# Top-32 attention with an MLP behind it: eight candidates of the smaller halves instead of sixteen, a second computation behind a branch, and 16 more units turned by VectorE

## The chip, the cores and the metric

The kernel runs on one core of a Trainium2 chip. A core has five instruction streams that matter here. TensorE (PE in the profile, with its weight loads as PEld) multiplies matrices. VectorE (DVE) does element-wise work, transposes of 32x32 blocks, and two special instructions for a top-k search: MAX8 gives the eight largest values of each row, and MATCH_REPLACE8 overwrites those eight in place. ScalarE (ACT) applies functions and copies out of PSUM. GpSimd (POOL) does element-wise work in SBUF. SyncE (SP) issues most DMAs. Each engine runs its own instructions in the order of the program, and semaphores hold an instruction until the others have produced what it reads. The metric is the device time of one execution in microseconds (us), as the median of several runs.

## What is computed

Eight batches, eight heads, 576 positions, head size 64, all in float32. For each row of the scores the 32nd largest is found, everything below it is masked, and the rest goes through a softmax and is multiplied with the values. The heads are then laid side by side and pass through a layer norm and an MLP with a hidden width of 2048 and a residual.

```python
scores = scale * np.matmul(q, k.transpose(0, 1, 3, 2))
kth = np.partition(scores, -top_k, axis=-1)[..., -top_k:-top_k + 1]     # top_k = 32
scores = np.where(scores >= kth, scores, -1000000000.0)
attn = np.exp(scores - np.max(scores, axis=-1, keepdims=True))
attn = attn / (np.sum(attn, axis=-1, keepdims=True) + 1e-09)
x = heads_side_by_side(np.matmul(attn, v))
xn = (x - mu) / np.sqrt(var + 1e-06) * g_ln
out = x + np.maximum(xn @ w_ch1, 0.0) @ w_ch2
```

## The kernel before

**Units.** The attention is cut into 160 units. A unit is a pair of heads of one batch with 128 query rows (a whole unit, two tiles of 128 rows by 576 keys, one for each head), or the last 64 rows of both heads in one tile (a rest unit). There are 128 whole units and 32 rest units, 288 tiles in all. Units are collected in groups of two or three that share their transposed weights `pt` and are multiplied with the values together.

**Top 32 of a row.** A row of 576 scores is folded: `halve` (L421) takes the larger of columns i and i+288 into `hi` (L433, on VectorE) and the smaller into `lo`. The smaller is made on GpSimd by two integer operations on the bits: a minus the larger, plus b (L438 and L441); only unit 0 uses a plain minimum on VectorE (L436). `select` (L443) then searches in four parts. Part 0 takes the sixteen largest of `lo` (MAX8 L453, MATCH_REPLACE8 L448, MAX8 L453) and puts them behind `hi`, which so gets 304 columns. Parts 1 to 3 run four rounds of MAX8 (L462) over the 304 columns with three rounds of MATCH_REPLACE8 (L448) between them. The last value of the fourth round is the 32nd largest of the row.

**Mask and softmax weights.** `mask` (L486) is one ScalarE instruction with the function Prelu and a slope of 2^-90 on the side of the values that are kept, so that kept and dropped values differ by a factor of 2^90. `weigh` (L493) is the exponential, with a scale that undoes the slope and a bias from `prepare` (L470: on VectorE for the first units, on GpSimd by two tiny operations, L483 and L484, from unit `CONVERTING` on); it sums the row as it goes.

**Turning the weights.** The weights have to be transposed for the product with the values. For most units TensorE does it with transposing matmuls (L553, L582), and ScalarE copies the result out of PSUM (L565, L583). For 72 units, those of batches 2 to 7 that are not a rest unit and not the last of their group, VectorE does it (`move`, L525: two STREAM_TRANSPOSE at L531 that write over the scores tile `sc`), and SP sends the blocks to HBM by one DMA (`turned`) and back into `pt` by four.

**Order.** The order is written out by hand. The program is a loop over steps; in step n each engine gets, in this order, the exponential of the first tile of unit n-2, the scores of unit n+2 (the products L412 on TensorE, four copies L393 to `sc` on ScalarE), the product of an older group with the values (L607, L614), the four parts of `select` for unit n, `halve` of unit n+1 between parts 1 and 2, and the two masks of unit n-1. During the first 8 units (`EARLY`) mask and exponential of a unit both stand in the same step, mask, exponential, mask, exponential. Matmuls of the MLP (L752, L909) are the filler: a list `todo` is spread over eight slots of a step. Up to `CONVERTING` a slot's share is the planner's VectorE cost of the step (`DVE_UNIT` 8.6 for a whole unit) less its TensorE cost; later it is what is left, spread evenly over the steps. In the first 17 or so steps the weights of the MLP are also converted, two pieces in a step: three or four ScalarE operations, a clamp on GpSimd (L197), a shift on VectorE (L200), and an addition and a product on GpSimd (L206, L208).

**Buffers.** Scores tiles `sc` have five buffers, `hi` two, `lo` one, the weights `e` two, `pt` one. The queues of the engines hold: on GpSimd the preparation of unit n-1, the halves of unit n+1, the sums of the MLP's blocks (L839 to L845, L889, L893, L723).

## Time and profile before

| what | us |
|---|---|
| time, median of 3 runs | 1653.51 (1651.67 to 1654.98) |
| time of the profiled execution | 1652.03 |
| span of the profiled execution | 1650.0 |
| TensorE busy | 1504.6 (91% of the span) |
| VectorE busy | 1458.2 (88%) |
| ScalarE busy | 1064.0 (64%) |
| GpSimd busy | 958.4 (58%) |
| mean granted TensorE clock | 0.959 of full speed |

A reader should look at three stages and not at the shares of the whole. Up to about 200 us the weights are converted and TensorE has little to do. From there to about 1490 us the 160 units run, with the MLP's matmuls as filler. After that VectorE is done with its units, and TensorE works off the last blocks of the MLP almost without a pause. In the lists below a row gives the source line, the engine, the operation, what it writes and reads, how often it ran, then busy time, mean duration of one, and the idle time before it with what ended it.

### The profile page before, as it was taken

The page shows a single profiled execution, that of the slowest core. Times are in us where ns is not written, and L with a number is a line of the kernel's source. Part 1 is how long each engine was busy: PE and PEld are TensorE (multiplying, and loading weights), DVE is VectorE, ACT ScalarE, POOL GpSimd, SP SyncE. Part 2 cuts the span into 40 slices and gives each one's busy share as a digit, 9 for nine tenths or more (in the row PEclk, how much of TensorE's full clock was granted, in tenths as well). Part 3 has the DMA queues.
Part 4 walks back from the last instruction along what each step waited for, and adds up shares of the span by engine and source line. Part 5 has one row for each costly group of instructions (what it writes and reads, how often), then busy time and mean ns, then how long its engine had stood idle before and what let it go on. Part 6 is the DMA issues. An engine that isn't in the chain of part 4 may idle for free.

```text
span 1650.0 us, 27871 instructions
## 1 busy us (share of the span) xinstructions
PE 1504.6 (91%) x7897; PEld 1134.6 (69%) x7897; DVE 1458.2 (88%) x4652; ACT 1064.0 (64%) x2712; POOL 958.4 (58%) x1492
## 2 busy tenths in 40 slices
PE   3569998999888988999999998999989999999998
PEld 1336566767655766777677776777767777778887
DVE  5999898999999999999999999999999999994000
ACT  6987876767655756667566665676657766654411
POOL 4778759555555564656564656474646564655243
PEclk6679999999999999999999999999999999999999
DMA  7533355113454455535555456535564455532211
GB/s 200 131 128 114 100 119 143 55 58 90 124 156 136 124 144 160 159 94 139 171 165 162 114 128 177 168 105 135 153 184 134 130 131 169 154 114 83 73 51 51
DMA packets 358945, 211.46 MB, mean 128 GB/s; under 512 B 250756, under 2 KB 331144, under 8 KB 358792
## 3 DMA queue, kind: packets, MB, share of 16 engines
q1 hardware_dynamic: 354056, 209.10, 44.9%
q10 hardware_dynamic: 4736, 0.59, 0.3%
q8 instruction: 63, 1.03, 0.3%
q14 instruction: 90, 0.74, 0.2%
HBM read 145.62 MB, written 63.96 MB: 127 GB/s over the span
## 4 chain that ended last, share of the span: by engine, by line
DVE 65%; PE 19%; POOL 7%; ACT 3%; DMA 2%; issue 2%; SPq 1%; DVEq 0%; POOLq 0%; ACTq 0%
DVE m L462 19%; DVE hi L448 17%; DVE hi L453 10%; PE hps L752 8%; PE ops L909 6%; DVE lo L448 6%; DVE hi L433 5%; DVE sc L531 4%; PE av L607 2%; PE scps L412 1%; POOL lo L441 1%; POOL lo L438 1%; DVE st L677 1%; DVE kT L342 1%; POOL w L208 1%
## 5 line engine op out<-in xcount | busy, mean ns | idle before, releaser
L752 PE MATMUL hps<-xT,w 128*128 128x256 f32 x2304 | 547.5, 383 | 1.9 <-ACT xT L714 1.9
L462 DVE MAX8 m<-hi 128x8 f32<-128x304 f32 x1152 | 489.5, 462 | 3.3
L752 PEld LDWEIGHTS hps<-xT,w 128*128 128x128 f32 x2304 | 422.0, 191 | 71.6 <-issue 15.4
L438 POOL TENSOR_TENSOR lo<-sc,hi 128x576 int32<-128x576 int32 (+1 forms) x159 | 204.5, 1286 | 451.3 <-DVE hi L433 224.3
L448 DVE MATCH_REPLACE8 hi<-m,hi 128x304 f32<-128x304 f32 x864 | 391.1, 460 | 0.0
L909 PE MATMUL ops<-w,h 128*128 128x256 f32 x1360 | 325.6, 383 | 1.7 <-POOL h L845 1.7
L909 PEld LDWEIGHTS ops<-w,h 128*128 128x128 f32 x1360 | 248.6, 191 | 42.9 <-issue 6.9
L453 DVE MAX8 hi<-lo 128x8 f32<-128x288 f32 x576 | 234.2, 443 | 7.5 <-POOL lo L441 6.4
L393 ACT COPY sc<-scps 128x288 f32<-128x288 f32 x576 | 195.8, 409 | 58.2 <-PE scps L412 21.0
L499 ACT ACTIVATE e<-e,bias 128x576 f32<-128x576 f32 x288 | 225.5, 783 | 9.6 <-POOL bias L484 9.0
L489 ACT ACTIVATE e<-sc,m 128x576 f32<-128x576 f32 x288 | 225.0, 782 | 5.8 <-DVE m L462 3.2
L441 POOL TENSOR_TENSOR lo<-lo,sc 128x576 int32<-128x576 int32 (+1 forms) x159 | 204.3, 1285 | 12.5
L607 PE MATMUL av<-pt,vb 128*64 128x256 f32 (+2 forms) x1088 | 158.1, 435 | 47.2 <-DMA pt<-turned 24.5
L607 PEld LDWEIGHTS av<-pt,vb 128*64 128x64 f32 x1088 | 81.6, 149 | 115.4 <-issue 42.2
L775 ACT ACTIVATE h<-hps 128x512 f32<-128x512 f32 x144 | 86.1, 598 | 115.8 <-PE hps L752 115.3
L412 PE MATMUL scps<-kT,late_qT 64*128 64x288 f32 (+3 forms) x832 | 128.7, 411 | 7.9 <-ACT pt L565 5.3
L909 PE MATMUL ops<-wt,s 128*128 128x256 f32 x544 | 129.2, 381 | 0.0
L448 DVE MATCH_REPLACE8 lo<-hi,lo 128x288 f32<-128x288 f32 x288 | 125.6, 443 | 0.0
L531 DVE STREAM_TRANSPOSE sc<-e 128x512 f32<-128x512 f32 x144 | 93.8, 685 | 35.0 <-ACT e L499 34.9
L433 DVE TENSOR_TENSOR hi<-sc 128x576 f32<-128x576 f32 (+1 forms) x160 | 110.8, 692 | 10.0 <-ACT sc L393 10.0
L553 PE MATMUL tp<-ident,e 128*128 128x128 f32 x576 | 91.7, 284 | 29.9 <-ACT e L499 28.3
L412 PE MATMUL scps<-kT,qT 64*128 64x288 f32 x512 | 92.3, 461 | 27.9 <-DVE qT L342 26.1
(96 smaller groups left out, 1843.9 us busy)
## 6 DMA issues: line engine op xcount, KB each, us to landing
turned<-sc SPq DMA_DIRECT2D x72, 512.0 KB, 2.6
pt<-turned SPq DMA_DIRECT2D x288, 128.0 KB, 2.9
w<-forms SPq DMA_DIRECT2D x136, 256.0 KB, 3.8
vb<-in_v_dram SPq DMA_DIRECT2D x136, 128.0 KB, 3.2
raw<-in_moe_w_ch_dram SPq DMA_DIRECT2D x32, 512.0 KB, 4.2
kT<-kept SPq DMA_DIRECT2D x36, 288.0 KB, 3.3
kin<-in_k_dram SPq DMA_DIRECT2D x128, 72.0 KB, 2.5
kept<-kT SPq DMA_DIRECT2D x32, 288.0 KB, 3.1
```

Source lines behind the costliest of these rows:

```text
L393: nc.scalar.copy(u.sc[:, t, s * HALF : (s + 1) * HALF], made[s][t][:, 0:HALF])
L412: nc.tensor.matmul(ps[i * R : i * R + ql, o : o + width], qT[r, q0 : q0 + ql], kT[r, k0 : k0 + width], start=True, stop=True,)
L438: nc.gpsimd.tensor_tensor(lo.bitcast(I32), a.bitcast(I32), hi.bitcast(I32), ALU.subtract)
L441: nc.gpsimd.tensor_tensor(lo.bitcast(I32), lo.bitcast(I32), b.bitcast(I32), ALU.add)
L448: nc.vector.match_replace(x[:, t], m[:, t, :], x[:, t], LOWEST)
L453: nc.vector.max(u.hi[:, t, o : o + 8], u.lo[:, t])
L462: nc.vector.max(m[:, t, :], u.hi[:, t])
L489: nc.scalar.activation(u.e[:, t], u.sc[:, t], AF.Prelu, bias=u.thr[:, t, 7:8], scale=-1.0, alpha=SLOPE)
L499: nc.scalar.activation(u.e[:, t], u.e[:, t], AF.Exp, bias=u.bias[:, t : t + 1], scale=-scale / SLOPE, accum_out=g.den[:, col : col + 1],)
L607: nc.tensor.matmul(av[h * D : (h + 1) * D, 0 : g.nq], vb[:, h * J + c, :], g.blocks[:, h, 0 : g.nq // 32, c, :], start=(c == 0), stop=False,)
L752: nc.tensor.matmul(ps[0][:, side * N : (side + 1) * N], w1[:, c, f * P : (f + 1) * P], self.xT[:, c, 0:N], start=(c == 0), stop=(c == NC - 1),
L909: nc.tensor.matmul(bank[name][:, 0:Q], a(j), rhs, start=first and j == 0, stop=(j == G - 1), skip_group_check=not first,)
```

## The change

The top-level function becomes `compute`, with two new arguments: `low_rounds`, the number of rounds over `lo`, and `doubt`, a one-element tile or nothing. The new top-level function calls it with one round, loads `doubt` into a register on every engine, and calls it again, with two rounds and no doubt, inside a branch that is taken only where `doubt` is 1. So the program holds two whole computations, one after the other.

- The search takes eight candidates of `lo` instead of sixteen: one MAX8 and no MATCH_REPLACE8 on `lo`. The first two rounds over `hi` now run on 288 columns, the last two on 296 (all four had 304).
- `halve` makes the smaller halves with a plain minimum on VectorE for every unit; GpSimd's two integer operations are gone.
- `mask` becomes a ScalarE Relu with a slope of 2^90 followed by a subtraction of the scores on GpSimd over the whole tile; the exponential reads the result. In the first 8 units the two masks now stand ahead of the two exponentials.
- `watch` notes for each unit, with one tiny operation, whether the eighth candidate reaches the row's 32nd value; every 16 units two short reductions on VectorE collect it (`settle_watch`), and at step N `tell` brings it to one number, with one transpose on TensorE.
- Bias and threshold of the mask are written into unused columns of the last round's tile, by two tiny operations as before.
- VectorE turns all units from `EARLY` on that are not a rest unit and not the last of their group: 88, of which 16 are new (4 of batch 0, 12 of batch 1).
- `DVE_UNIT` in the planner becomes 7.65 and the rest unit's cost 0.58 of that. Two small tiles change pools.

```diff
     nt = len(u.tiles)
     u.lo = lopool.tile([P, 2, HALF], FP32, tag="lo", name="lo")
-    u.hi = hipool.tile([P, 2, HALF + TOP_K // 2], FP32, tag="hi", name="hi")
+    u.hi = hipool.tile([P, 2, HALF + 8 * low_rounds], FP32, tag="hi", name="hi")
     nc.vector.tensor_tensor(hi, a, b, ALU.max)
-    if u.i == 0:
-        nc.vector.tensor_tensor(lo, a, b, ALU.min)
-        return
-    nc.gpsimd.tensor_tensor(lo.bitcast(I32), a.bitcast(I32), hi.bitcast(I32), ALU.subtract)
-    nc.gpsimd.tensor_tensor(lo.bitcast(I32), lo.bitcast(I32), b.bitcast(I32), ALU.add)
+    nc.vector.tensor_tensor(lo, a, b, ALU.min)
...
 def select(u, i):
-    if i == 0:
-        for o in range(HALF, HALF + TOP_K // 2, 8):
-            for t in nt:
-                nc.vector.max(u.hi[:, t, o : o + 8], u.lo[:, t])
-            if o == HALF:
-                for t in nt:
-                    replace(u.hi[:, :, o : o + 8], t, u.lo)
-        return
-    for r in ((0,), (1,), (2, 3))[i - 1]:
-        ...
+    if i == 1:
+        for r in range(low_rounds):
+            o = HALF + 8 * r
+            for t in nt:
+                nc.vector.max(u.hi[:, t, o : o + 8], u.lo[:, t])
+            ...
+    width = HALF + 8 * low_rounds if i > 1 else HALF
+    for t in nt:
+        nc.vector.max(m[:, t, :], u.hi[:, t, 0:width])
+    if i < TOP_K // 8 - 1:
+        for t in nt:
+            replace(m, t, u.hi[:, t, 0:width])
...
 def prepare(u):
+    u.bias, u.edge = u.thr[:, 0:nt, 5], u.thr[:, 0:nt, 6]
+    if doubt is not None:
+        watch(u)
+    eng = nc.vector if u.i < CONVERTING else nc.gpsimd
+    eng.tensor_scalar(u.edge, u.thr[:, 0:nt, 7], STEEP, 0.0, ALU.mult, ALU.add)
+    eng.tensor_scalar(u.bias, u.top[:, 0:nt, 0], -scale, 0.0, ALU.mult, ALU.add)
...
+def watch(u):
+    c = 1 + 2 * (u.i % 16)
+    eng = nc.vector if u.i < CONVERTING else nc.gpsimd
+    eng.tensor_tensor(watched[:, c : c + nt], u.hi[:, 0:nt, HALF + 7], u.thr[:, 0:nt, 7], ALU.subtract)
...
 def mask(u, t):
     nc.scalar.activation(
-        u.e[:, t], u.sc[:, t], AF.Prelu, bias=u.thr[:, t, 7:8], scale=-1.0, alpha=SLOPE
+        u.e[:, t], u.sc[:, t], AF.Relu, bias=u.edge[:, t : t + 1], scale=-STEEP
     )
+    nc.gpsimd.tensor_tensor(u.e[:, t], u.e[:, t], u.sc[:, t], ALU.subtract)
...
-for u in units[jobs[5 * NHP].first :]:
+for u in units[EARLY:]:
     u.moved = not u.rest and u is not u.group.units[-1]
...
-DVE_UNIT, DVE_REST, DVE_MOVE, DVE_TURN = 8.6, 5.0, 1.4, 1.45
+DVE_UNIT = 6.0 + 1.65 * low_rounds
+DVE_REST, DVE_MOVE, DVE_TURN = 0.58 * DVE_UNIT, 1.4, 1.45
...
     if early:
         for t in range(2):
             mask(ex, t)
+        for t in range(2):
             weigh(ex, t)
...
+    if doubt is not None and at(n - 1) and at(n - 1).ends_watch:
+        settle_watch()
+        if n == N:
+            tell()
...
+    doubt = ctx.enter_context(tc.tile_pool(name="doubt", bufs=1)).tile([1, 1], I32, tag="doubt", name="doubt")
+    compute(tc, *operands, low_rounds=1, doubt=doubt[:])
+    again = nc.values_load(doubt[:], min_val=0, max_val=1, ...)
+    with tc.If(again > 0):
+        compute(tc, *operands, low_rounds=2, doubt=None)
```

More of the change, by code (lines that the diff above doesn't have):

```diff
@@ L19 @@
 DEN_EPS = 1.0e-9
-SLOPE = 2.0**-90
+STEEP = 2.0**90
 LN_EPS = 1.0e-6
@@ L29, with compute @@
 @with_exitstack
-def kernel(
+def compute(
     ctx: ExitStack,
@@ L39 @@
     out: bass.AP,
+    low_rounds: int,
+    doubt: bass.AP | None,
 ):
@@ L136 @@
         nc.gpsimd.memset(t[:], 0.0)
+    if doubt is not None:
+        watched = const([P, 34], "watched")
+        nc.gpsimd.memset(watched[:], -1.0)
     ident = const([P, P], "ident")
@@ L372, in __init__ @@
             self.tiles = [(0, 1)] if self.rest else [(0,), (1,)]
-            self.moved = False
+            self.moved = self.ends_watch = False
             self.e = None
@@ L433, in halve @@
         nc.vector.tensor_tensor(hi, a, b, ALU.max)
-        if u.i == 0:
-            nc.vector.tensor_tensor(lo, a, b, ALU.min)
-            return
-        nc.gpsimd.tensor_tensor(
-            lo.bitcast(I32), a.bitcast(I32), hi.bitcast(I32), ALU.subtract
-        )
-        nc.gpsimd.tensor_tensor(lo.bitcast(I32), lo.bitcast(I32), b.bitcast(I32), ALU.add)
+        nc.vector.tensor_tensor(lo, a, b, ALU.min)
     def select(u, i):
@@ L447, in replace @@
         def replace(m, t, x):
-            nc.vector.match_replace(x[:, t], m[:, t, :], x[:, t], LOWEST)
-        if i == 0:
-            for o in range(HALF, HALF + TOP_K // 2, 8):
+            nc.vector.match_replace(x, m[:, t, :], x, LOWEST)
+        if i == 1:
+            for r in range(low_rounds):
+                o = HALF + 8 * r
                 for t in nt:
                     nc.vector.max(u.hi[:, t, o : o + 8], u.lo[:, t])
-                if o == HALF:
+                if r < low_rounds - 1:
@@ L455, in select @@
                     for t in nt:
-                        replace(u.hi[:, :, o : o + 8], t, u.lo)
-            return
-        for r in ((0,), (1,), (2, 3))[i - 1]:
-            pl = brief_small if r in (1, 2) else small
-            m = pl.tile([P, 2, 8], FP32, tag=f"m{r}", name=f"m{r}")
-            for t in nt:
-                nc.vector.max(m[:, t, :], u.hi[:, t])
-            if r < TOP_K // 8 - 1:
-                for t in nt:
-                    replace(m, t, u.hi)
-            if r == 0:
-                u.top = m
-            u.thr = m
+                        replace(u.hi[:, :, o : o + 8], t, u.lo[:, t])
@@ L470, in prepare @@
+        width = HALF + 8 * low_rounds if i > 1 else HALF
+        pl = brief_small if i in (1, 2) else small
+        m = pl.tile([P, 2, 8], FP32, tag=f"m{i}", name=f"m{i}")
+        for t in nt:
+            nc.vector.max(m[:, t, :], u.hi[:, t, 0:width])
+        if i < TOP_K // 8 - 1:
+            for t in nt:
+                replace(m, t, u.hi[:, t, 0:width])
+        if i == 0:
+            u.top = m
+        u.thr = m
     def prepare(u):
         nt = len(u.tiles)
-        u.bias = small.tile([P, 2], FP32, tag="bias", name="bias")
@@ L474, in prepare @@
-        b = u.bias[:, 0:nt]
-        if u.i < CONVERTING:
-            for t in range(nt):
-                nc.vector.tensor_scalar(
-                    b[:, t : t + 1], u.thr[:, t, 7:8], u.top[:, t, 0:1], scale,
-                    ALU.subtract, ALU.mult,
-                )
-            return
-        nc.gpsimd.tensor_tensor(b, u.thr[:, 0:nt, 7], u.top[:, 0:nt, 0], ALU.subtract)
-        nc.gpsimd.tensor_scalar(b, b, scale, 0.0, ALU.mult, ALU.add)
+        u.bias, u.edge = u.thr[:, 0:nt, 5], u.thr[:, 0:nt, 6]
@@ new lines, in prepare @@
+        if doubt is not None:
+            watch(u)
[3 more added lines that the diff above has]
+    def watch(u):
+        nt = len(u.tiles)
+        c = 1 + 2 * (u.i % 16)
+        eng = nc.vector if u.i < CONVERTING else nc.gpsimd
+        eng.tensor_tensor(
+            watched[:, c : c + nt], u.hi[:, 0:nt, HALF + 7], u.thr[:, 0:nt, 7], ALU.subtract
+        )
+        if u.i % 16 == 15 or u.i == N - 1:
+            u.ends_watch = True
@@ new lines, in settle_watch, with tell @@
+    def settle_watch():
+        for out, first, op in ((0, 0, ALU.max), (33, 1, ALU.min)):
+            nc.vector.tensor_reduce(
+                watched[:, out : out + 1], watched[:, first : first + 33],
+                mybir.AxisListType.X, op,
+            )
+    def tell():
+        w = hpool.tile([P, J * P], FP32, tag="h", name="tell")
+        nc.gpsimd.memset(w[:], 0.0)
+        nc.vector.tensor_scalar(w[:, 1:2], watched[:, 33:34], -1.0e38, None, ALU.is_le)
+        nc.vector.tensor_scalar(w[:, 0:1], watched[:, 0:1], 0.0, None, ALU.is_ge)
+        nc.vector.tensor_tensor(w[:, 0:1], w[:, 0:1], w[:, 1:2], ALU.max)
+        ps = brief("tell")
+        nc.tensor.transpose(ps[:, 0:P], w[:, 0:P], ident[:])
+        nc.vector.tensor_reduce(w[0:1, P : P + 1], ps[0:1, 0:P], mybir.AxisListType.X, ALU.max)
+        nc.vector.tensor_copy(doubt, w[0:1, P : P + 1])
@@ L499, in weigh @@
         nc.scalar.activation(
-            u.e[:, t], u.e[:, t], AF.Exp, bias=u.bias[:, t : t + 1], scale=-scale / SLOPE,
+            u.e[:, t], u.e[:, t], AF.Exp, bias=u.bias[:, t : t + 1], scale=-scale,
             accum_out=g.den[:, col : col + 1],
@@ L675, in stats @@
                 self.rstd = small.tile([P, J], FP32, tag="rstd", name="rstd")
-            st = small.tile([P, 6], FP32, tag="st", name="st")
+            st = brief_small.tile([P, 6], FP32, tag="st", name="st")
             nc.vector.bn_stats(out=st[:], in_=x)
@@ L681, in stats @@
             else:
-                less = small.tile([P, 1], FP32, tag="less", name="less")
+                less = brief_small.tile([P, 1], FP32, tag="less", name="less")
                 nc.gpsimd.tensor_scalar(
@@ L1317, with kernel @@
             pop()
+@with_exitstack
+def kernel(
+    ctx: ExitStack,
+    tc: tile.TileContext,
+    *operands: bass.AP,
+):
+    nc = tc.nc
+    doubt = ctx.enter_context(tc.tile_pool(name="doubt", bufs=1)).tile(
+        [1, 1], I32, tag="doubt", name="doubt"
+    )
+    compute(tc, *operands, low_rounds=1, doubt=doubt[:])
+    again = nc.values_load(
+        doubt[:], min_val=0, max_val=1,
+        skip_runtime_bounds_check_because="a comparison's result",
+    )
+    with tc.If(again > 0):
+        compute(tc, *operands, low_rounds=2, doubt=None)
 _INS = ['q', 'k', 'v', 'moe_g_ln', 'moe_w_ch1', 'moe_w_ch2']
```

## The prediction

> **What bounds the kernel now.** I read the busy times first, then the stages, then the waits of the bound engine, then single rows.

> The page's busy line, then three stretches of the span: their length, the busy time of each engine in the order PE, PEld, DVE, ACT, POOL, the granted clock, DMA share and GB/s.

> ```profile
> PE 1504.6 (91%) x7897; PEld 1134.6 (69%) x7897; DVE 1458.2 (88%) x4652; ACT 1064.0 (64%) x2712; POOL 958.4 (58%) x1492
> ```

> ```profile
> 0.00:200.00 200.00, 132.82 (x582) 84.02 (x583) 172.44 (x566) 163.53 (x364) 143.90 (x136) 0.80 0.49 139
> 200.00:1490.00 1290.00, 1218.68 (x6564) 918.81 (x6563) 1267.83 (x4033) 851.58 (x2240) 750.40 (x1232) 0.98 0.48 135
> 1490.00:1650.00 160.00, 153.10 (x753) 131.79 (x753) 17.97 (x55) 48.88 (x110) 64.08 (x126) 0.99 0.21 63
> ```

> From 200 to 1490 us VectorE is busy 98.3% of the time (1267.8 of 1290) and TensorE 94.5% (1218.7). VectorE is the bound, but TensorE follows 49 us behind: whatever VectorE is spared beyond that is worth nothing in this stretch. Before 200 us TensorE idles for 67 us, and VectorE, ScalarE and GpSimd share the bound. After 1490 us TensorE alone works.

> What TensorE waits for between 500 and 1450 us, and what GpSimd waits for over the span (total, times, longest):

> ```profile
> PE av L607 <- DMA pt<-turned: 17.7, 10, 4.7
> PE av L607 <- ACT sc L393: 5.9, 2, 5.0
> PE av L607 <- DMA kept<-late_qT: 5.2, 1, 5.2
> ```

> ```profile
> POOL lo L438 <- DVE hi L433: 224.3, 64, 5.4
> POOL lo L438 <- DVE den L1238: 139.7, 54, 4.1
> ```

> TensorE's waits are mostly for data that VectorE delivered late, and should shrink with its load. The last two rows matter more than they seem: GpSimd waits for VectorE, behind its maximum, in most units, so it is idle while that maximum runs. The change removes this order.

> What it may cost shows in one place, around 254 us (the timeline: start, duration, engine):

> ```profile
> 253.83 1.28 POOL L962 TENSOR_TENSOR wt<-w 128x512 f32<-128x512 f32 x1
> ...
> 254.57 1.17 DVE L433 TENSOR_TENSOR hi<-sc 128x576 f32<-128x576 f32 x1
> 255.20 1.67 POOL L963 TENSOR_TENSOR wt<-w,wt 128x512 f32<-128x512 f32 x1
> ```

> Nearly every other maximum on 576 columns takes 0.74 to 0.76 us. This one starts while GpSimd runs an operation of the same kind, takes 1.17 us and ends 0.63 us after that operation, so that most of its own 0.75 lies behind it; GpSimd's next one takes 1.67 us where its like take 1.28. Two-input operations of the two engines seem to run one after the other.

> **The change, part by part.** Durations are from the groups of instructions, which follow.

> ```profile
> L462 DVE MAX8 m<-hi 128x8 f32<-128x304 f32 x1152 | 489.5, 462 | 3.3
> L448 DVE MATCH_REPLACE8 hi<-m,hi 128x304 f32<-128x304 f32 x864 | 391.1, 460 | 0.0
> L453 DVE MAX8 hi<-lo 128x8 f32<-128x288 f32 x576 | 234.2, 443 | 7.5 <-POOL lo L441 6.4
> L448 DVE MATCH_REPLACE8 lo<-hi,lo 128x288 f32<-128x288 f32 x288 | 125.6, 443 | 0.0
> L448 DVE MATCH_VALUE_LOAD lo<-hi,lo 128x8 f32 x288 | 22.8, 79 | 1.1
> L433 DVE TENSOR_TENSOR hi<-sc 128x576 f32<-128x576 f32 (+1 forms) x160 | 110.8, 692 | 10.0 <-ACT sc L393 10.0
> L531 DVE STREAM_TRANSPOSE sc<-e 128x512 f32<-128x512 f32 x144 | 93.8, 685 | 35.0 <-ACT e L499 34.9
> L553 PE MATMUL tp<-ident,e 128*128 128x128 f32 x576 | 91.7, 284 | 29.9 <-ACT e L499 28.3
> ```

> *Search.* One of two MAX8 over `lo` goes: 234.2/2 = 117.1 us. MATCH_REPLACE8 over `lo` goes with its loads: 125.6 + 22.8 = 148.4. Sixteen columns are worth 19 ns in a MAX8 (462 less 443) and 17 in a replacement, so the narrower `hi` saves 288 x (2x19 + 2x9.5 + 2x17 + 8.5) ns = 28.6. Sum 294.1 us of VectorE.

> *Minimum on VectorE.* As many and as large as the maximum: +110.8 us. Net of both, 183.3 us less over 160 units; 143 units are prepared by GpSimd after 200 us (its row at L483 counts 143), so 183.3 x 143/160 = 163.8 fall in the long stretch.

> *Sixteen more units turned.* VectorE +2 x 0.651 us each (93.8/144), 12 of them after 200 us: +15.6. TensorE loses eight transposes a unit, 91.7/576 = 0.159 each: 12 x 8 x 0.159 = 15.3 us. ScalarE loses 32 copies of 0.58, hidden before and after. SP gets five DMAs a unit, 80 of some 0.45 us; they land in 2.6 and 2.9 us, and the conversion's fetches queue behind them. A fetch is issued a step (10 us) ahead and lands in 4.2, so this costs nothing unless the step's end slips by 5 us.

> *Watch.* Every 16 units two reductions of some 0.2 us, +4 us on VectorE. One more 0.2 us operation a unit on GpSimd, +29. VectorE's maximum of unit n+1 now waits until GpSimd has watched unit n-1 (`hi` has two buffers). Behind it queue the whole next unit; GpSimd reaches the watch early in its step, so I take 0, the other end being the 2.6 us that its bias waited at most.

> *Mask.* GpSimd loses L438 and L441 (204.5 + 204.3 = 408.8) and gains 288 subtractions. The nearest row is its 576-column integer operation at 1.41 us: 406. So GpSimd's load stays. But each exponential now waits for GpSimd. In the steady part the subtraction stands half a step (4 to 5 us) ahead of its exponential: 0, as long as GpSimd is not that late. In the first 8 units it stands directly ahead: mask 0.78, subtraction 1.41, exponential; ScalarE waits about 0.65 and then 0.45 us, 1.1 a unit. From 60 to 110 us ScalarE is busy 47.2 of 50, 9.6 of a 10.2 us step, so its step becomes 10.7: +4 us over 8 steps, against up to 0.5 a step that VectorE saves in the next nine. I take +2 for the first 200 us, ends -8 and +12.

> *Side by side.* This is the large unknown. VectorE now runs two two-input operations a unit with GpSimd free to run beside them, busy about 0.6 of the time. The row above paid 0.42 us. A first operation meets GpSimd in 0.6 of cases and waits about half of an operation (0.5, over 1.41, 1.27 and 0.46 us operations): 0.3. The second either follows at once (0) or GpSimd, held back meanwhile, goes first (0.6 x 0.85 = 0.5): 0.25. I take 0.55 us a unit, 79 us over 143 units. Ends: 0, as in most rows now, and 2 x 0.6 x 1.41 = 1.7 us, 243 in all.

> [...]

> *Branch.* Each engine loads a register and jumps over a second program. No row shows it; the nearest are DMA landings of 2.4 to 5.1 us. I take +4, ends 0 and 10. In these inputs no row has more than six of its top 32 among the smaller halves, so the second computation should not run. [...]

> *Planner and tail.* The smaller `DVE_UNIT` and the moved units change the filler of steps 9 to 17 in opposite directions; the order of TensorE's matmuls is nearly the same. `tell` puts one transpose behind VectorE near the end: +2.

> **Sum.** VectorE in the long stretch: 1267.8 - 163.8 + 15.6 + 4 + 79 = 1203 us. TensorE: 1218.7 - 15.3 = 1203, less some 10 if half of its waits go, since the product with the values takes up to 4.5 us behind such a wait and 1.9 otherwise: 1193. Two engines with the same load that wait for each other fill less than 98.3% and more than 94.5%; with 96.5%, 1203 becomes 1246. So -44, and +2 +2 +4: 1650.0 - 36 = 1614 us of span. The profiled run took 2.0 more than its span and lies 1.5 under the median; I say **1615 us**. Its own range, with 0.3 to 0.8 us a unit, is 1592 to 1640.

> **Rivals.** *TensorE alone is the bound*: the engines hardly meet. VectorE needs 1124 us, TensorE 1193; at 98.5% that is 1211, and 1650 - 79 + 8 + 2 = **1581**. For it: TensorE hardly idles in the last stretch, where VectorE is out of the way. Against it: GpSimd is no longer held back by the maximum.

> *Waiting side by side costs more than the search saves* (slower). Without any gain VectorE could do 1282 x 0.983 = 1260 us, 136 more than 1124: break-even at 0.95 us a unit. At 1.2 us, 1296/0.983 = 1318, or 1650 + 28 + 8 + 2 = **1688**. For it: GpSimd's new 1.41 us operations. Against it: the single row paid 0.42.

> *GpSimd holds ScalarE*: exponentials wait in the steady part too, the scores' copies queue behind them and TensorE idles as now; 0.3 us a step in 150 steps eats the 44 and leaves the other 8: 1650 + 1 + 8 + 2 = **1661**. For it: the exponential waited for GpSimd's bias three times, up to 4.7 us, and GpSimd is busy 19.3 of 20 us around 250. Against it: 58% on average.

> **How the numbers follow.** Forecast 0.50, TensorE bound 0.25, side by side 0.18, GpSimd 0.07. The forecast is faster but for 0.03 that ends within 0.2%, TensorE's case always; the two others are slower: 0.72, 0.03 and 0.25. 0.2% (3.3 us) is about what a measurement can tell. The range takes in the forecast's own, most of TensorE's case and half of the slow one: 1568 to 1690 leaves out about a third of the 0.25 below and half of the 0.18 above, 0.17.

> **What the profile after would show.** [...] The maximum's and minimum's mean: 0.69 if they never meet GpSimd, 0.95 by my value, above 1.15 if slower. TensorE above 96% from 200 us on. Exponentials waiting for the subtraction: some 9 us early and few later. I am wrong if the mean of the two operations is off, or if ScalarE's waits for GpSimd exceed 40 us.

## The result

The changed kernel takes 1666.5 us, the median of four runs (1662.9 to 1669.3), against 1652.9 us of the kernel before on the same chip: 1.0084 times as long, with an interval of 1.0071 to 1.0096. It is 0.8% slower. I had forecast 1615 us and faster. The time lies inside my range, but on the other side of the kernel before.

The profiled execution took 1662.9 us, with a span of 1661.1. First the page's busy line after the change, then the same three stretches as in the prediction (length, busy time of PE, PEld, DVE, ACT and POOL, granted clock, DMA share, GB/s).

```profile
PE 1499.4 (90%) x7770; PEld 1124.9 (68%) x7770; DVE 1357.2 (82%) x4022; ACT 1051.2 (63%) x2680; POOL 1078.2 (65%) x1607
```

```profile
0.00:200.00 200.00, 120.91 (x484) 75.93 (x485) 160.79 (x458) 147.48 (x324) 133.59 (x121) 0.82 0.48 137
200.00:1490.00 1290.00, 1217.10 (x6494) 910.55 (x6493) 1173.23 (x3491) 850.74 (x2239) 862.98 (x1341) 0.98 0.50 147
1490.00:1650.00 160.00, 160.00 (x790) 137.52 (x789) 23.16 (x74) 51.77 (x116) 77.89 (x143) 1.00 0.23 68
```

VectorE lost its load as planned: in the long stretch it is busy for 1173.2 us instead of 1267.8, 91% of the time. But TensorE does no more there than before (1217.1 against 1218.7 us), and it does 12 us less in the first 200. No engine is busy all the time now; the engines wait for each other. The page's groups show for whom (busy time, mean ns of one, then the idle time before it and what ended most of it):

```profile
L484 POOL TENSOR_TENSOR e<-e,sc 128x576 f32<-128x576 f32 x288 | 411.6, 1433 | 418.1 <-ACT e L481 407.5
...
L429 DVE MAX8 m<-hi 128x8 f32<-128x296 f32 (+1 forms) x1152 | 465.0, 443 | 1.1
L415 DVE MATCH_REPLACE8 hi<-m,hi 128x288 f32<-128x288 f32 (+1 forms) x864 | 378.4, 444 | 0.0
...
L492 ACT ACTIVATE e<-e,m 128x576 f32<-128x576 f32 x288 | 225.0, 781 | 69.6 <-POOL e L484 69.2
L407 DVE TENSOR_TENSOR hi<-sc 128x576 f32<-128x576 f32 (+1 forms) x160 | 123.3, 771 | 142.1 <-POOL watched L452 120.8
...
L408 DVE TENSOR_TENSOR lo<-sc 128x576 f32<-128x576 f32 (+1 forms) x160 | 122.1, 763 | 0.0
L524 DVE STREAM_TRANSPOSE sc<-e 128x512 f32<-128x512 f32 x176 | 113.9, 682 | 7.4 <-ACT e L492 7.4
...
L421 DVE MAX8 hi<-lo 128x8 f32<-128x288 f32 x288 | 118.0, 446 | 0.0
L546 PE MATMUL tp<-ident,e 128*128 128x128 f32 x448 | 75.2, 294 | 47.1 <-ACT e L492 46.9
```

Read the last column as a ring. GpSimd's subtraction waits for ScalarE's mask (407.5 us; before, GpSimd waited for VectorE's maximum). ScalarE's exponential waits for GpSimd's subtraction (69.2). TensorE's transposes wait for the exponential (46.9; before 28.3). And VectorE's maximum waits for GpSimd's watch (120.8 us; before, this wait did not exist).

**How the loss builds up.** I took the start of the maximum of each unit from VectorE's timeline and subtracted its start in the kernel before. The differences in us, worked out so for several kernels (units 0 to 7 are the early ones):

| kernel | unit 5 | 10 | 23 | 47 | 79 | 119 | 151 |
|---|---|---|---|---|---|---|---|
| after | +2.6 | +19.3 | +23.5 | +31.1 | +19.4 | +13.9 | +10.8 |
| no_subtract_early | -1.7 | -1.9 | +1.5 | +10.1 | +3.5 | -1.8 | -4.2 |
| no_watch | +2.4 | +19.8 | +18.2 | +19.9 | -2.6 | -13.4 | -18.2 |
| neither_wait | -3.7 | -2.4 | -4.1 | +1.4 | -14.4 | -25.2 | -29.8 |
| no_guard_prelu | -3.8 | -2.8 | -16.6 | -28.3 | -50.0 | -61.4 | -66.9 |

After the change the kernel is 19 us late by unit 10, at about 140 us. It loses 12 more until unit 47 and wins 20 back until unit 151, where a kernel without guard and subtraction wins 67. The first place of the loss is the part in which mask, subtraction and exponential of a unit stand in one step. One such step from the timeline (start, duration, engine; in brackets the idle time before and what ended it):

```profile
96.37 1.46 ACT L481 ACTIVATE e<-sc,m 128x576 f32<-128x576 f32 x2
96.53 0.76 DVE L407 TENSOR_TENSOR hi<-sc 128x576 f32<-128x576 f32 x1 [3.05 <-ACT sc L367]
97.20 0.75 DVE L408 TENSOR_TENSOR lo<-sc 128x576 f32<-128x576 f32 x1
97.24 3.33 POOL L484 TENSOR_TENSOR e<-e,sc 128x576 f32<-128x576 f32 x2 [1.30 <-ACT e L481]
...
99.24 0.78 ACT L492 ACTIVATE e<-e,m 128x576 f32<-128x576 f32 x1 [1.42 <-POOL e L484]
...
100.17 1.11 PE L546 MATMUL tp<-ident,e 128*128 128x128 f32 x4 [4.70 <-ACT e L492]
...
100.61 0.78 ACT L492 ACTIVATE e<-e,m 128x576 f32<-128x576 f32 x1 [0.50 <-POOL e L484]
```

The scores' copies release ScalarE's masks and VectorE's two halves within 0.2 us of each other, so in this step, and in the last five of the eight early ones, GpSimd's subtractions begin while VectorE is at the minimum. The two take 3.33 us together, where twice the usual 1.41 would be 2.8. The first exponential starts 2.0 us after the subtraction began, and the last at 100.61, 4.2 us after the first mask; in the kernel before, mask and exponential follow each other on ScalarE without a gap (95.42 and 96.23). TensorE stands for 4.70 us. From the maximum of unit 6 to that of unit 9 (84.39 to 122.12 us) a step takes 12.6 us in the mean; in the kernel before it takes 9.6 (79.88 to 108.54). VectorE is not what holds these steps: it waits 3.05 us for the copies of the next scores.

The second place is in the steady part, and it runs through four engines. The longest case but one, which comes at the very end of the units, is around 1233 us:

```profile
1231.19 0.44 DVE L415 MATCH_REPLACE8 hi<-m,hi 128x288 f32<-128x288 f32 x1
1233.07 0.43 ACT L615 COPY oT<-av 128x320 f32<-128x320 f32 x1 [8.16 <-PE av L607]
1233.39 0.78 ACT L481 ACTIVATE e<-sc,m 128x576 f32<-128x576 f32 x1
1234.25 1.41 POOL L484 TENSOR_TENSOR e<-e,sc 128x576 f32<-128x576 f32 x1 [8.61 <-ACT e L481]
...
1238.37 0.78 ACT L481 ACTIVATE e<-sc,m 128x576 f32<-128x576 f32 x1
...
1239.22 1.41 POOL L484 TENSOR_TENSOR e<-e,sc 128x576 f32<-128x576 f32 x1 [3.39 <-ACT e L481]
...
1240.59 0.19 POOL L452 TENSOR_TENSOR watched<-hi,m 128x1 f32<-128x1 f32 x1
1240.81 0.76 DVE L407 TENSOR_TENSOR hi<-sc 128x576 f32<-128x576 f32 x1 [9.18 <-POOL watched L452]
```

ScalarE waits 8.16 us for the product with the values, and both masks stand behind that copy. GpSimd waits for each mask (8.61 and 3.39 us) before it can subtract. The watch, 0.19 us long and with all its data ready, stands behind the second subtraction in GpSimd's queue. And VectorE, which needs the buffer that the watch reads, is idle for 9.18 us. The maximum itself has nothing to do with the masks that it waits for.

### The profile page after: what moved, and what is told of

It is laid out like the page before. It is cut to its first block, busy times and chain, and to the rows that moved or that the text cites. A ratio compares the mean times of both kernels' runs of the same rounds, so it can differ in the third digit from the quotient of the medians.

```text
span 1661.1 us, 27307 instructions
## 1 busy us (share of the span) xinstructions
PE 1499.4 (90%) x7770; PEld 1124.9 (68%) x7770; DVE 1357.2 (82%) x4022; ACT 1051.2 (63%) x2680; POOL 1078.2 (65%) x1607
## 4 chain that ended last, share of the span: by engine, by line
PE 56%; DVE 20%; POOL 8%; DMA 6%; ACT 5%; issue 3%; SPq 2%; DVEq 0%; ACTq 0%; POOLq 0%
PE hps L745 21%; PE ops L902 16%; PE av L600 6%; PE scps L386 6%; DVE m L429 6%; DVE hi L415 5%; POOL e L484 3%; DMA turned<-sc 2%; DVE lo L408 2%; DVE sc L524 2%; PE av L607 2%; DMA pt<-turned 2%; PE tp L546 2%; DVE hi L407 1%; DVE hi L421 1%
## 5 line engine op out<-in xcount | busy, mean ns | idle before, releaser
L484 POOL TENSOR_TENSOR e<-e,sc 128x576 f32<-128x576 f32 x288 | 411.6, 1433 | 418.1 <-ACT e L481 407.5
L429 DVE MAX8 m<-hi 128x8 f32<-128x296 f32 (+1 forms) x1152 | 465.0, 443 | 1.1
L415 DVE MATCH_REPLACE8 hi<-m,hi 128x288 f32<-128x288 f32 (+1 forms) x864 | 378.4, 444 | 0.0
L492 ACT ACTIVATE e<-e,m 128x576 f32<-128x576 f32 x288 | 225.0, 781 | 69.6 <-POOL e L484 69.2
L407 DVE TENSOR_TENSOR hi<-sc 128x576 f32<-128x576 f32 (+1 forms) x160 | 123.3, 771 | 142.1 <-POOL watched L452 120.8
L481 ACT ACTIVATE e<-sc,m 128x576 f32<-128x576 f32 x288 | 223.8, 781 | 15.3 <-POOL m L444 14.5
L408 DVE TENSOR_TENSOR lo<-sc 128x576 f32<-128x576 f32 (+1 forms) x160 | 122.1, 763 | 0.0
L524 DVE STREAM_TRANSPOSE sc<-e 128x512 f32<-128x512 f32 x176 | 113.9, 682 | 7.4 <-ACT e L492 7.4
L386 PE MATMUL scps<-kT,qT 64*128 64x288 f32 x512 | 93.7, 468 | 27.7 <-ACT sign L168 11.8
L421 DVE MAX8 hi<-lo 128x8 f32<-128x288 f32 x288 | 118.0, 446 | 0.0
L546 PE MATMUL tp<-ident,e 128*128 128x128 f32 x448 | 75.2, 294 | 47.1 <-ACT e L492 46.9
L386 PEld LDWEIGHTS scps<-kT,late_qT 64*128 64x128 f32 (+1 forms) x832 | 72.2, 170 | 58.5 <-issue 24.6
```

Source lines behind the costliest of these rows:

```text
L386: nc.tensor.matmul(ps[i * R : i * R + ql, o : o + width], qT[r, q0 : q0 + ql], kT[r, k0 : k0 + width], start=True, stop=True,)
L408: nc.vector.tensor_tensor(lo, a, b, ALU.min)
L415: nc.vector.match_replace(x, m[:, t, :], x, LOWEST)
L429: nc.vector.max(m[:, t, :], u.hi[:, t, 0:width])
L481: nc.scalar.activation(u.e[:, t], u.sc[:, t], AF.Relu, bias=u.edge[:, t : t + 1], scale=-STEEP)
L484: nc.gpsimd.tensor_tensor(u.e[:, t], u.e[:, t], u.sc[:, t], ALU.subtract)
```

## The experiments

My theory after this reading: the loss is the sum of two new waits, the first units' subtraction between mask and exponential, and the maximum's wait for the watch. The rival: VectorE and GpSimd run their two-input operations one after the other, as in the prediction's large unknown, and the waits only show it. Kernels are edits of the changed kernel, unless said otherwise; times are medians, ratios are to the kernel before on the same chip, with 95% intervals.

### The subtraction: of the first units, and of all

```diff
-        nc.gpsimd.tensor_tensor(u.e[:, t], u.e[:, t], u.sc[:, t], ALU.subtract)
+        if not (u.i < EARLY):      # no_subtract_early;  no_subtract: never
+            nc.gpsimd.tensor_tensor(u.e[:, t], u.e[:, t], u.sc[:, t], ALU.subtract)
```

> The changed kernel without GpSimd's subtraction in the first 8 units (their exponentials read the Relu's result directly, so the weights of those units are left wrong); all else as it is. Theory A (the early chain mask, GpSimd, exponential costs about 20 us by unit 10, because the subtraction runs beside VectorE's two halves): about 18 us less than the changed kernel, 1648 us, and unit 10's maximum starts within 3 us of where the kernel before has it (121 us, against 140 in the changed kernel). Rival B (the early loss comes from elsewhere: VectorE's tiny operations, the order of the masks): within 5 us of the changed kernel, 1662 to 1670.

> The changed kernel without GpSimd's subtraction in all units (the weights are left wrong everywhere; 411 us of GpSimd's 1078 go). Theory A (everything that is lost comes through GpSimd: the early chain, and later VectorE's and ScalarE's waits for GpSimd's queue): 18 us from the early stage and 20 or more from the waits behind it, 1620 to 1630 us, and VectorE's wait for the watch falls from 121 us below 40. Rival C (TensorE is the bound after 200 us, and the waits are only idle time of engines with slack): no more than the early 18 us, 1645 to 1650.

Without the first units' subtractions: 1645.5 us, 0.9952 (0.9933 to 0.9972), 21 us less than after. In the table above they are the 21.2 us between the two kernels at unit 10; from there to unit 47 both lose 12 us. So the subtraction of the first units costs 21 us, where I had put +2; the new order of the masks and VectorE's tiny operations, which this kernel keeps, cost nothing there. Without any subtraction: 1588.7 us, 0.9609 (0.9580 to 0.9638), far below the 1620 to 1630 that I expected. With the subtractions the wait for the watch goes too, although the watch is still made:

```profile
L407 DVE TENSOR_TENSOR hi<-sc 128x576 f32<-128x576 f32 (+1 forms) x160 | 117.8, 736 | 32.7 <-POOL watched L452 27.7 <-ACT sc L367 4.9
```

From 120.8 to 27.7 us: the watch is late because it stands behind the subtractions, which stand behind ScalarE's masks.

### The guard: watch, branch and second program

```diff
-    compute(tc, *operands, low_rounds=1, doubt=doubt[:])
-    again = nc.values_load(doubt[:], ...)
-    with tc.If(again > 0):
-        compute(tc, *operands, low_rounds=2, doubt=None)
+    compute(tc, *operands, low_rounds=1, doubt=None)        # no_watch
+    compute(tc, *operands, low_rounds=1, doubt=doubt[:])    # no_branch: watch and tell stay
...
```

> The changed kernel without the watch, the branch and the second computation (the guard against rows that need more candidates is left out). Theory D (VectorE's 121 us of waiting for GpSimd's watch is where the search's gain went): 25 us or more less, below 1642 us. Theory C (VectorE waits because it runs ahead of TensorE, and branch and second program cost little): 2 to 8 us less, 1658 to 1664.

> The changed kernel with the watch and the one number in place, but without loading it, the branch and the second computation (left out). Theory D: 0 to 6 us less than the changed kernel, 1660 to 1666. Rival E (the second program behind the branch is what costs): some 25 us less, about 1640.

Without the guard: 1636.7 us, 0.9914 (0.9884 to 0.9943), 30 us less than after. Without the branch and the second program alone: 1663.0 us, 1.0056 (1.0037 to 1.0074), 3.4 less than after, hardly more than the measurement can tell. That is about what I had put down for the branch (4 us), and some 26 us are the watch, with what collects it and its own time on GpSimd. Where the wait for the watch is taken away, two other things grow. This is VectorE in no_watch:

```profile
L407 DVE TENSOR_TENSOR hi<-sc 128x576 f32<-128x576 f32 (+1 forms) x160 | 149.8, 936 | 26.4 <-ACT sc L367 26.3
L408 DVE TENSOR_TENSOR lo<-sc 128x576 f32<-128x576 f32 (+1 forms) x160 | 127.8, 799 | 0.0
L524 DVE STREAM_TRANSPOSE sc<-e 128x512 f32<-128x512 f32 x176 | 117.1, 689 | 81.9 <-ACT e L492 65.0 <-POOL e L484 16.5
```

The maximum and the minimum take 936 and 799 ns instead of 771 and 763, and the stream transposes wait 81.9 us, not 7.4, most of it for exponentials that are late. I take it that the 120.8 us of waiting were worth only about 26 us of time because most of them covered these.

### The watch on VectorE

```diff
-        eng = nc.vector if u.i < CONVERTING else nc.gpsimd
-        eng.tensor_tensor(
+        nc.vector.tensor_tensor(                    # issued right behind select(u, 3)
             watched[:, c : c + nt], u.hi[:, 0:nt, HALF + 7], u.thr[:, 0:nt, 7], ALU.subtract
         )
...
```

> The changed kernel with the watch's one tiny operation on VectorE behind the last round for every unit (as the first 17 units have it anyway), so that VectorE's maximum of unit n+1 no longer waits for GpSimd's queue; guard, branch and second computation stay. Theory D (that wait took the gain): it costs VectorE 143 x 0.2 = 29 us that it has to spare, and gives most of what leaving the whole guard out gave (30 us): 1638 to 1648 us. Rival E (the branch and the second program cost it): 1660 or more.

1653.9 us, 1.0004 (0.9992 to 1.0017): 13 us less than after, and less of a gain than expected. The wait is gone, but the operation on two columns took 343 ns in the mean, 55.0 us over 160 units: 159 ns at the least, 165 in the median, and up to 1390 where it met a GpSimd operation.

### The search alone, the new halves, and the turning

before_with_eight is the kernel before, with the search cut to eight candidates and nothing else changed; no_guard_prelu is the changed kernel without guard and with the one-instruction mask of before; turn_72 is the changed kernel with the 72 turned units of before.

```diff
 # before_with_eight, in select of the kernel before
-            for o in range(HALF, HALF + TOP_K // 2, 8):
-                for t in nt:
-                    nc.vector.max(u.hi[:, t, o : o + 8], u.lo[:, t])
-                if o == HALF: ... replace(u.hi[:, :, o : o + 8], t, u.lo)
+            for t in nt:
+                nc.vector.max(u.hi[:, t, HALF : HALF + 8], u.lo[:, t])
...    (and the tile of hi has 296 columns)
 # no_guard_prelu, besides the lines of no_watch
-            u.e[:, t], u.sc[:, t], AF.Relu, bias=u.edge[:, t : t + 1], scale=-STEEP
-        nc.gpsimd.tensor_tensor(u.e[:, t], u.e[:, t], u.sc[:, t], ALU.subtract)
+            u.e[:, t], u.sc[:, t], AF.Prelu, bias=u.thr[:, t, 7:8], scale=-1.0, alpha=SLOPE
...    (and bias and scale of the exponential as before)
 # turn_72
-    for u in units[EARLY:]:
+    for u in units[jobs[5 * NHP].first :]:
```

> The kernel before with the eight candidates alone: one MAX8 of the smaller halves, 296 columns in all four rounds, nothing else changed (the guard against rows that need more is left out). VectorE loses some 117 + 148 + 9 us. If TensorE is the bound behind VectorE (its 145 us of idle time, 49 of them between 200 and 1490 us), 25 to 50 us less than before, 1600 to 1628 us. If the search's time on VectorE is worth its full amount, 1500 us or less. If other waits take its place at once, 1645 or more.

> The changed kernel without the guard (left out) and with the mask of the kernel before (one Prelu, no subtraction on GpSimd); minimum on VectorE and 88 units turned by VectorE as in the changed kernel. Theory A+D (the subtraction and the watch's wait explain the whole loss against the kernel before with eight candidates, 1579 us): 1570 to 1588 us. Rival F (the minimum on VectorE or the 16 more turned units cost too): 1595 or more.

> The changed kernel with 72 units turned by VectorE instead of 88. Theory A+D (the 16 units are not the cause): within 5 us of the changed kernel, 1661 to 1671. Rival F (turning them on VectorE, five DMAs each, costs the 11 us that the changed kernel loses between units 17 and 47): 1652 to 1658 us.

before_with_eight: 1578.7 us, 0.9551 (0.9523 to 0.9579). The smaller search alone is worth 73 us, more than the 25 to 50 that I gave for the case that TensorE is the bound, and TensorE is the bound then (over the span it idles 89.1 us instead of 145.4 and is busy for 15.6 less): in its long stretch

```profile
200.00:1490.00 1290.00, 1269.41 (x6919) 969.70 (x6918) 1070.47 (x3314) 884.38 (x2306) 787.17 (x1283) 1.00 0.50 139
```

TensorE is busy for 1269.4 of 1290 us, 98.4%, and VectorE for 83%. The prediction's rival "TensorE alone is the bound" has 98.5% and 1581 us. It was worked out for the whole change, with 15 us less work for TensorE and 8 us more for mask, branch and tail, so the nearness of the two times is in part luck.

no_guard_prelu: 1580.8 us, 0.9562 (0.9546 to 0.9578), not told apart from before_with_eight. The two differ in the minimum (on VectorE, with GpSimd's two operations a unit gone), the 16 turned units, the planner's costs, the order of the search, 8 columns in its first two rounds, and a few tiny operations. All this together costs nothing when VectorE has room.

turn_72: 1655.1 us, 1.0022 (1.0010 to 1.0034), 11 us less than after. That is the range of the rival in the expectation. In the changed kernel the 16 turned units do cost something. By which way stays open: the stream transposes wait as little for late exponentials in turn_72 (7.3 us) as in after (7.4), while TensorE waits 37.5 us before its transposes instead of 47.1 and ScalarE's exponentials 52.0 us for GpSimd instead of 69.2.

### Two waits or one, and the meeting of VectorE and GpSimd

neither_wait leaves out the guard and the first units' subtractions. subtract_aside and meeting_alone (the latter without guard) keep GpSimd's subtraction in its place, and take away its result:

```diff
-        nc.gpsimd.tensor_tensor(u.e[:, t], u.e[:, t], u.sc[:, t], ALU.subtract)
+        nc.gpsimd.tensor_tensor(u.sc[:, t], u.sc[:, t], u.sc[:, t], ALU.subtract)
```

> Guard (watch, branch, second program) left out, and the subtraction of the first units (up to the tenth job) left out with it. If the early chain (-21 us) and the watch (-30 us) are two separate losses, they add up: 1666.5 - 21 - 30 = 1615.5, so 1610 to 1621, which is about the time that I predicted for the whole change. If they are one and the same late start, told twice, the two together give little more than one: 1630 to 1637. What is left above the time without subtraction and guard (near 1581) is what the subtraction costs from the ninth unit on.

> GpSimd's subtraction keeps its place, its size and its two inputs from SBUF, but it subtracts the scores from themselves and writes over the scores, so the exponential reads ScalarE's own mask and waits for nothing of GpSimd (the kept weights of a row all become equal; the rest is computed as after). Theory 1: what the subtraction costs is ScalarE's wait for it; GpSimd's load and its meetings with VectorE cost little. Then the time comes near that of the kernel without any subtraction (1588.7 us): 1588 to 1610, with the maximum and the minimum still at 0.75 us or more. Theory 2: the subtraction costs through GpSimd's load and through VectorE's operations that run beside it (the maximum that waits for the watch, behind the subtractions in GpSimd's queue, included); then the early units' chain is gone, but the rest stays: 1635 to 1655.

> No guard, and GpSimd's subtraction as in subtract_aside: it keeps GpSimd as busy and meets VectorE's operations as before, but nothing waits for its result but the turning that follows the exponential anyway (the kept weights of a row become equal). Without guard and without subtraction the time was 1580.8 us, with the subtraction of the later units and ScalarE's waits for it 1616.75. Theory 1: what is left there is the exponentials' waits for GpSimd; then 1581 to 1593. Theory 2: it is VectorE's operations waiting beside GpSimd's, which no wait in the trace names; then 1604 to 1617, with the maximum and minimum together at 1.7 us or more a unit.

neither_wait: 1616.8 us, 0.9769 (0.9737 to 0.9801). The two losses add up: 1666.5 - 29.8 - 20.9 = 1615.8. They are two separate things.

One thing differs from what the expectations say: GpSimd isn't kept quite as busy. Taking a buffer from itself took 1147 ns in the median there, the real subtraction 1411 in after, a difference of some 75 us over the kernel. So what falls away in these two kernels is the wait for the result and a part of GpSimd's load.

subtract_aside: 1635.7 us, 0.9895 (0.9865 to 0.9924), at the lower end of what the second theory gave and far from the first. Against no_subtract_early (1645.5), the exponentials' waits in the steady part and that part of the load are worth 10 us; VectorE still waits 114.9 us for the watch.

meeting_alone: 1604.6 us, 0.9709 (0.9688 to 0.9731). This is the second theory's range, at its lower end. From neither_wait it is 12 us less, again for the exponentials' waits and the shorter subtraction (1477 ns in the mean there); and 24 us more than no_guard_prelu, the price of GpSimd's subtractions, in this shorter form, merely being run. The subtraction, and the two halves, which in no_guard_prelu take 757 and 775 ns:

```profile
L484 POOL TENSOR_TENSOR sc<-sc 128x576 f32<-128x576 f32 x288 | 353.7, 1231 | 496.0 <-ACT e L481 493.7
...
L407 DVE TENSOR_TENSOR hi<-sc 128x576 f32<-128x576 f32 (+1 forms) x160 | 139.3, 871 | 6.9 <-ACT sc L367 6.9
L408 DVE TENSOR_TENSOR lo<-sc 128x576 f32<-128x576 f32 (+1 forms) x160 | 128.8, 805 | 0.0
```

The halves take 0.14 us more a unit, 23 us of VectorE. It is a part of the 24, but not all need be: 12 of the 24 are lost before unit 23, in the part where GpSimd also converts weights: the maximum of unit 23 starts 5.0 us earlier than in the kernel before, and that of no_guard_prelu 16.6. How much of these is GpSimd's load and how much the meeting stays open.

### A version that keeps the guard

The watch needs the eighth candidate after the search has gone on. So I copied it out of the large buffer, first with a COPY, then with a reduction over the eight candidates; guarded_best and guarded_reduced also make the first units' subtractions on VectorE and turn 72 units.

```diff
 def select(u, i):  # behind the MAX8 of lo, in i == 1
+            u.eighth = small.tile([P, 2, 1], FP32, tag="eighth", name="eighth")
+            nc.vector.tensor_copy(u.eighth[:, 0:nt], u.hi[:, 0:nt, HALF + 7 : HALF + 8])        # eighth_copied
+            nc.vector.tensor_reduce(u.eighth[:, 0:nt, 0], u.hi[:, 0:nt, HALF : HALF + 8], X, ALU.min)  # eighth_reduced
 def watch(u):
-            watched[:, c : c + nt], u.hi[:, 0:nt, HALF + 7], u.thr[:, 0:nt, 7], ALU.subtract
+            watched[:, c : c + nt], u.eighth[:, 0:nt, 0], u.thr[:, 0:nt, 7], ALU.subtract
 def mask(u, t):    # guarded_best, guarded_reduced
-        nc.gpsimd.tensor_tensor(u.e[:, t], u.e[:, t], u.sc[:, t], ALU.subtract)
+        eng = nc.vector if u.i < EARLY else nc.gpsimd
+        eng.tensor_tensor(u.e[:, t], u.e[:, t], u.sc[:, t], ALU.subtract)
```

> VectorE copies the eighth candidate of the smaller halves into a small buffer of its own as soon as it is found, and GpSimd's watch reads the copy; so the larger halves' buffer is free when VectorE has searched it, and the maximum of unit n+1 waits for nothing of GpSimd. Guard, branch and second program stay. Theory: 27 of the guard's 30 us are the maximum's wait for the watch. The copy adds some 0.15 us a unit to VectorE (the 128x2 TENSOR_SCALARs took 0.14 to 0.5), 24 us, of which half shows: 1640 to 1650, and no row of the maximum waiting for the watch. Rival: the wait is only moved, since VectorE then waits at the turning for the exponentials, and the copy is paid in full: 1655 to 1668.

> A kernel that computes all that after computes, guard and second program included: the eighth candidate is copied (as in eighth_copied), the subtraction of the first units (up to the tenth job) is made by VectorE in place of GpSimd, at 0.75 us each, and 72 units are turned as before. If the three losses are separate, 1666.5 - (20 to 25) - (10 to 21) - (5 to 11) = 1610 to 1632, faster than both kernels. If VectorE is now the bound again through the copies and the early subtractions (some 24 + 27 us more), 1640 to 1655, no faster or little faster than before.

> As eighth_copied (guard, branch and second program kept, the watch reads a small buffer), but VectorE fills that buffer with one TENSOR_REDUCE (the minimum of the unit's eight candidates) and not with a COPY. In eighth_copied the COPY took 153 ns at least, 170 in the median and 1432 at most, while no MAX8, replacement, reciprocal, stream transpose or reduction ever took over 10% more than its median. Theory: a COPY waits for GpSimd like a TENSOR_TENSOR, a TENSOR_REDUCE does not; then the new row means 0.16 to 0.19 us (28 us in all, where the COPY took 56) and the time falls by 15 to 28 us: 1627 to 1640. Rival: the time of the small operation is hidden by other waits, or moves to the minimum and maximum, and the time stays within 6 us of eighth_copied: 1649 to 1661.

> guarded_best with the TENSOR_REDUCE in place of the COPY; it computes all that after computes. By the first theory of eighth_reduced 1637.1 - (15 to 28) = 1609 to 1622; by its rival 1631 to 1643.

eighth_copied: 1655.1 us, 1.0016 (1.0003 to 1.0028), the rival's range. No maximum waits for the watch any more, but the copy of two columns cost 56 us. The trace of one line gives its shortest, median and longest duration in ns; first the copy in eighth_copied, then the reduction in eighth_reduced:

```profile
L427 DVE COPY eighth<-hi x160: 153/170/1432, 15.3 to 1516.1; 128x2 f32<-128x2 f32 x128, 128x1 f32<-128x1 f32 x32
```

```profile
L427 DVE TENSOR_REDUCE eighth<-hi x160: 160/170/171, 14.9 to 1499.1; 128x2 f32<-128x16 f32 x128, 128x1 f32<-128x8 f32 x32
```

Both take 170 ns in the median; the copy took up to 1432, as long as GpSimd's subtraction, and the reduction never more than 171. The five longest copies each ended 22 to 25 ns after a subtraction of GpSimd; the 50 copies that began outside any GpSimd operation took 172 ns at most. Of the reductions 103 began inside a GpSimd operation, and none was longer for it. In the mean copy and reduction took 350 and 168 ns. The reduction thus spares VectorE 29 us, as I expected, and by medians the kernel gains 6 of them: 1649.2 us, 0.9977 (0.9962 to 0.9992), which is the rival's range again, at its lower end. So in these two runs the COPY over two columns waited beside GpSimd and the TENSOR_REDUCE didn't, but most of what VectorE was spared didn't reach the time. In the trace the stream transposes wait 47.7 us for their data, 37.0 in eighth_copied. The traced execution was the fastest of ten, though (1640.2 us), so where the rest goes is not shown.

The copies over one column, those of the rest units, are an exception that the lines above hide:

```profile
L427 DVE COPY eighth<-hi 128x1 f32<-128x1 f32 x32 | 4.9, 154 | 1.1
```

25 of these 32 began inside a GpSimd operation, and none took more than 156 ns; those over two columns took 399 in the mean. Two copies of one column each, in place of one of two, were not tried.

With the first units' subtractions on VectorE and 72 turned units it counts for more: guarded_best took 1637.1 us, 0.9909 (0.9883 to 0.9935), and guarded_reduced 1624.6 us, 0.9828 (0.9811 to 0.9845), 12.5 less, though both lie between the two ranges expected. guarded_reduced computes all that the changed kernel computes, the guard and the second program included, and is faster than both kernels: by 1.7% than before and by 42 us than after. A guard beside the one-instruction mask, and a third buffer for `hi`, were not tried.

## Why the prediction was wrong

**The account.** By medians, from the changed kernel downwards: the guard 29.8 us (after to no_watch), the first units' chain 20.0 (to neither_wait), the exponentials' later waits 12.2 (to meeting_alone), GpSimd's subtractions merely being run 23.8 (to no_guard_prelu), minimum and turned units 2.1 (to before_with_eight, within the measurement). These are 88 us. The smaller search alone gave 74 against the 1652.9 of the same comparison. The difference is the 14 us that the change lost. Such a row of differences closes whatever its parts are. That the first two are separate is shown by taking them out singly and together; the cut between 12.2 and 23.8 is rough, since the subtraction in meeting_alone is the shorter one, and only their sum, 36.0, is firm.

*Search* was right: MAX8 and MATCH_REPLACE8 took 1263.2 us before (489.5 + 391.1 + 234.2 + 125.6 + 22.8, the loads of the rounds over `hi` left out in both) and 961.4 after (465.0 + 378.4 + 118.0), 301.8 less, where I had 294.1. What it is worth was nearly right in the rival that makes TensorE the bound, 1581 us against 1578.7, in part by luck, as said above.

*Minimum on VectorE* (110.8 us, measured 122.1), *Sixteen more units turned* (113.9 - 93.8 = 20.1 us of VectorE, 16.5 less of TensorE) and *Branch* (4, measured 3.4, hardly more than the measurement can tell) were right in size. The 11 us that the turned units cost in the changed kernel I had not. And a small slip: a span of 1614 us with the 2.0 and 1.5 that I named gives 1617.5, not 1615.

***Mask* failed in the first units.** I put them at "+2 for the first 200 us, ends -8 and +12", from 1.1 us a unit of ScalarE's waiting, and set VectorE's savings against it. The runs showed 20. I had missed that the subtraction begins beside VectorE's minimum, in five of the eight steps, and takes longer there (1.96 to 1.97 us in after, where 1.41 is usual): 3.33 us for two, not 2.8, and ScalarE waits 1.42 + 0.50 = 1.92 us a unit. Above all I had counted ScalarE's load, where a chain sets the step: mask, subtraction, exponential, transposes on TensorE (which stand for 4.70 us), the next scores, their copies, the next mask. VectorE's savings, which I set against it, were not on this chain. Of the 3 us that a step grew, ScalarE's waits explain 1.9; the rest I did not trace.

***Watch* failed.** "GpSimd reaches the watch early in its step, so I take 0, the other end being the 2.6 us" was read from a trace in which GpSimd's queue stood behind VectorE's maximum. The change put it behind ScalarE's masks. The watch of a unit stands behind the subtractions of the unit before it, and VectorE waited for it 57 times, 120.8 us in all and up to 11.4. The watch as a whole costs some 26 us (no_branch to no_watch). Where a reduction takes this wait away, at 27 us of VectorE, the time falls by 17 (eighth_reduced).

***Mask* in the steady part** was taken as "0, as long as GpSimd is not that late". It is late: ScalarE waited 48.3 of its 69.2 us for GpSimd after 140 us, worth at most some 10 to 12 us. My own bound (wrong if these waits exceed 40 us) caught this.

***Side by side* was not what I missed; its size was high for this kernel.** I took 79 us of VectorE, which made the time 34 us longer than the rival without it (1615 and 1581); the nearest measure is the 24 us of meeting_alone. The halves took 123.3 + 122.1 us, against 2 x 110.8 at the mean of before: 24 us more. With the watch's wait removed it is 149.8 + 127.8 - 221.6 = 56. My estimate counted the two halves alone, but they were not all that took longer beside GpSimd: the COPY over two columns took up to 1432 ns in eighth_copied, 170 in the median, while the COPY over one column took 156 at the most.

Of the signs I had named, the halves' mean of 0.77 us is near "never meet" (0.69). TensorE reached 94.3% of the long stretch, not 96%. The nearest case was the rival to which I gave the least chance, *GpSimd holds ScalarE*, at 1661 us. Its mechanism was half right: GpSimd came late, but it held VectorE, through a buffer, more than it held ScalarE.

## What to carry to other kernels

An engine that is busy for 58% of the time is not free for 42% of it: its queue is in order, so an operation of 0.2 us is as late as the latest producer of what stands ahead of it (here the watch, 0.19 us long, for which VectorE was idle 9.18 us), and before anything is put on such a queue one asks whose results its neighbours wait for. When a tiny reader keeps a large buffer from being reused, give it a small buffer of its own: here that took 17 us off the time (after to eighth_reduced). And price a change by its parts: here the search gave 74 us, and the mask and the guard that came with it took 86.

## What the hardware showed that I had not expected

```profile
L434 DVE MAX8 m<-hi x1152: 407/445/471, 12.8 to 1519.7; 128x8 f32<-128x296 f32 x102, 128x8 f32<-128x288 f32 x90
```

MATCH_REPLACE8 (432/443/458), STREAM_TRANSPOSE (656/687/712), BATCH_NORM_STATS2 (660/676/695), RECIPROCAL (164/166/180) and TENSOR_REDUCE (150/174/189) behaved alike. The first kind is TENSOR_TENSOR (the maximum in after: 758 ns in the median, up to 1957), and COPY and TENSOR_SCALAR over two columns or more, in eighth_copied the bias among them: 154 ns at the least, 160 in the median, 1386 at the most. Over one column TENSOR_TENSOR still waited (up to 1111 ns in watch_on_vectore), but COPY didn't, as shown above, nor did TENSOR_SCALAR: in the kernel before, 31 of the 33 that make the bias began inside a GpSimd operation, and none took more than 215 ns, 207 in the median. So here one reduction did a two-column copy's work in half of its mean time (168 against 350 ns).
